# An mLSTM layer with a feed-forward network on one core: how the three-part operands of the late chunks are built

## Chip, core and metric

The kernel runs on one core of a Trainium2 chip. The metric is the device time of one execution in microseconds (us). TensorE is called PE in the profile, VectorE DVE, ScalarE ACT, GpSimd POOL, and SyncE, which issues nearly all DMAs, SP.

## The reference

Inputs are q, k, v and o_gate of shape (4, 8, 768, 40) (batch, heads, tokens, head size) and i_gate and f_gate of shape (4, 8, 768). Token by token, with a running maximum m that keeps the exponentials small:

```
m_new = max(f + m, i)
C = exp(f + m - m_new) * C + exp(i - m_new) * v k^T
n = exp(f + m - m_new) * n + exp(i - m_new) * k
y = sigmoid(o_gate) * (C q) / max(|n q|, 1)
```

The heads are joined to x of shape (3072, 320), and the network follows: h = x w_in (320 x 2048), g = max(h, 0) + alpha min(h, 0), out = g w_out (2048 x 320).

## The kernel before, in words

**Chunks and groups.** The recurrence is done in chunks of 128 tokens: 4 batches of NC = 6 chunks, n = 0 to 23. Two chunks (GC = 2) make a group of 256 tokens, and the network runs group by group, 12 groups. Within a chunk the weights between tokens are a masked matrix of scores (k against q, per head, times exponentials of the gates, tile E), and what came before the chunk enters through the state C.

**Precision.** Products are made from operands split into high and low parts. In the network x, the weights and g are split in two parts (XH and XL, WH and WL, OH and OL, gh and gl). In chunks n >= NDIR = 7, q and k are split into three bf16 parts, and the three parts of a head stand one above the other as 3 x 40 = 120 rows, so that one matmul adds three products of parts. Two such stacks of q, with the parts in other slots, against two of k give the six products that matter; `stage_b` (L410) issues the two matmuls per head at L443, and `from_state` (L358) does the same with stacks of q against two stacks of the state (L372).

**How the stacks are made now.** `token_parts(n, j)` (L220; j = 0 for q, 1 for k) fills a block by token, tile Z (names qZ and kZ): 128 tokens x 2 stacks x 8 heads x 128 columns, of which three slots of 40 hold the parts and 8 are zero (the memset at L231). ACT writes the first part to its slot in both stacks at once (L235). The remainder, tile `rest` (names qr and kr), is a subtraction at L236, for q on POOL and for k on DVE. ACT writes the second part (L238), DVE the third (L239), and DVE copies the first and the second part into the slots that are still open (L241, L242). One DMA transpose (L244) turns the block, 2048 columns, into the tile qS or kS with 120 rows in use. The block of q has the tag `sp0`, that of k the tag `sp1`, one buffer each, so a block can be written again only when the transpose of the chunk before has read it. The same two tags hold the split g of group 1 in the network's first part (names gg, L595). `stage_s` (L291) runs the two iterators: both first phases, a yield, the rest of q, a yield, the rest of k.

**State.** After each chunk `update_steps` (L149) and `state` (L184) bring C up to date, and from batch 1 on `state` splits it into three parts too, 40 rows of 336: ACT copies (L203, L205), a subtraction on DVE (L204) and one on POOL (L206), and three DMAs (L207 to L209) that place the parts in the other rows of the two stacks. The scratch tile `cw` shares the tag `qf` (two buffers) with `rest`.

**Order.** `attention` (L513) walks the chunks. In step n it issues `loads(n + 2)` (q, k, every second time v, and `load_L`, the row of gates that is spread over 128 partitions, 512 KB), runs `stage_s(n + 2)` as `far` and `stage_b(n)` as `bb`, and ends with `after(n + 1)`, which updates the state and splits v (`value_parts`, L317). The tuple at L524 says in which order their pieces come. The network of an earlier group is issued between these pieces (`ffn`, L646; `FeedForward.up`, L569; `down`, L603): per pair of blocks of 128 features `up` issues 16 matmuls into a buffer in PSUM (two buffers), ACT makes the negative part (L587), DVE the activation (L591, twice), ACT the high part gh (L599), POOL the low part gl (L600), and two pairs later `down` issues 12 matmuls (L608). Each engine carries out its queue in order. The order within a queue is set at build time by the framework's scheduler, which follows the program's order and may bring work forward that it reckons to be ready. The last two groups of the network run after the last chunk.

Of the kernel before, what the change touches and what calls it, by code (L numbers as in the profile page):

```python
# [8 lines left out]
F32 = mybir.dt.float32  # L9
F32R = mybir.dt.float32r  # L10
U32 = mybir.dt.uint32
BF16 = mybir.dt.bfloat16
# [5 lines left out]
def kernel(ctx: ExitStack, tc: tile.TileContext, q, k, v, i_gate, f_gate, o_gate, w_in, w_out, alpha, out):  # L18
    nc = tc.nc
# [75 lines left out]
    def by_token_of(n, j):  # L95

        t = (qn_t, kn_t)[j][n % NQ]
        if n < NDIR:
            return t[:, :, :D]
        return t.rearrange("p h e -> p (h e)")[:, : H * D].rearrange("p (h e) -> p h e", e=D)  # L100
# [83 lines left out]
    def state(n, pu):  # L184


        b, c = divmod(n, NC)
        C = C_t[0][:D]
        if c > 0:
            nc.gpsimd.tensor_tensor(  # L190
                C, C, gamB[:D, b * H : (b + 1) * H, c : c + 1].broadcast_to([D, H, VA]), ALU.mult
            )
        for par in range(2):
            to, new = by_parity(C, par), by_parity(pu[64 * par : 64 * par + D], par)
            if c == 0:
                nc.vector.tensor_copy(to, new)
            else:
                nc.vector.tensor_tensor(to, to, new, ALU.add)
        X = state_parts(n)
        C = C.rearrange("p h e -> p (h e)")  # L200
        cw = sb.tile([P, 512], F32, tag="qf", name=f"cw{n}")
        rest, low = cw[:D, : H * VA], cw[:D, H * VA :].bitcast(BF16)[:, : H * VA]
        nc.scalar.copy(X[:D, 0], C)  # L203
        nc.vector.tensor_tensor(rest, C, X[:D, 0], ALU.subtract)  # L204
        nc.scalar.copy(X[:D, 1], rest)  # L205
        nc.gpsimd.tensor_tensor(low, rest, X[:D, 1], ALU.subtract)  # L206
        nc.sync.dma_start(X[D : 2 * D], X[:D])  # L207
        nc.sync.dma_start(X[2 * D : 3 * D, 1], X[:D, 0])
        nc.sync.dma_start(X[2 * D : 3 * D, 0], low)  # L209

    def state_parts(n):

# [4 lines left out]
        for p in range(NPR):  # L217
            nc.tensor.transpose(ps[:R, p * P : (p + 1) * P], src[:, p * P : p * P + R], ident)

    def token_parts(n, j):  # L220

        src = by_token_of(n, j)
        Z = sb.tile([P, 2, H, P], BF16, tag=f"sp{j}", name=f"{'qk'[j]}Z{n}", bufs=1)
        rest = sb.tile([P, H, D], F32, tag="qf", name=f"{'qk'[j]}r{n}")

        def slot(block, i):
            return Z[:, block, :, i * D : (i + 1) * D]

        nc.gpsimd.memset(Z[:, :, :, 3 * D :], 0.0)  # L231
        flat = Z.rearrange("p s h x -> p (s h x)")
        W = H * P + 2 * D
        both = bass.AP(flat.tensor, flat.offset, [list(flat.ap[0]), [W, 2], [P, H], [1, D]])
        nc.scalar.copy(both, src.unsqueeze(1).broadcast_to([P, 2, H, D]))  # L235
        (nc.gpsimd, nc.vector)[j].tensor_tensor(rest, src, slot(0, 0), ALU.subtract)  # L236
        yield
        nc.scalar.copy(slot(1, 1), rest)  # L238
        nc.vector.tensor_tensor(slot(0, 2), rest, slot(1, 1), ALU.subtract)  # L239

        nc.vector.tensor_copy(slot(1 - j, 1 - (1 - j)), slot(0, 0))  # L241
        nc.vector.tensor_copy(slot(j, 1 - j), slot(1, 1))  # L242
        X = sb.tile([P, 2 * H, P], BF16, tag="qk"[j] + "S", name=f"{'qk'[j]}S{n}")
        nc.sync.dma_start_transpose(X, flat)  # L244
        stacks[n, j] = X.rearrange("p (s h) t -> p s h t", s=2)
        yield

    stacks = {}

    kpads = []  # L250

# [32 lines left out]
    def after(n):  # L284

        update(n)
        if n >= NBF:
            for _ in value_parts(n):
                pass

    def stage_s(n):  # L291

        parts = [token_parts(n, j) for j in range(2)]
        for it in parts:
            next(it)
        yield
        next(parts[0])
        yield
        next(parts[1])
        chunk[n] = (stacks.pop((n, 0)), stacks.pop((n, 1)), None)  # L300
        yield

    def values(n, E, busy=lambda: None):

# [53 lines left out]
    def from_state(n, qf, Q=None):  # L358

        b, c = divmod(n, NC)  # L360
        pI = psa(f"pI{n}")
        if b == 0:
            C = C_t[(n - 1) % 3][:R].rearrange("p h e -> p (h e)")
            for p in range(NPR):
                es = slice(2 * p * VA, 2 * (p + 1) * VA)
                nc.tensor.matmul(pI[:, es], qf[:R, p * P : (p + 1) * P], C[:, es], start=True, stop=True)
        else:
            C = state_parts(n - 1)[: 3 * D]
            for h in range(H):
                es = slice(h * VA, (h + 1) * VA)  # L370
                for s in range(2):
                    nc.tensor.matmul(pI[:, es], Q[: 3 * D, s, h], C[:, 1 - s, es], start=s == 0, stop=s == 1)  # L372
        yield
        T = sb.tile([P, H, VA], F32, tag="T", name=f"T{n}")
        nc.vector.tensor_tensor(
            T, pI[:, : H * VA].rearrange("p (h e) -> p h e", e=VA),
            eT[:, c, b * H : (b + 1) * H].unsqueeze(2).broadcast_to([P, H, VA]), ALU.mult,
        )
        yield T
# [30 lines left out]
    def stage_b(n):  # L410

        b, c = divmod(n, NC)
        Lb, (Q, K, qf) = pre.pop(n), chunk.pop(n)
        Es = []
        for par in range(2):
            E = sb.tile([P, 512], F32, tag="E", name=f"E{n}_{par}", bufs=4)
            if Lb is None:
                pb = psa(f"pb{n}_{par}")
                for p in range(NPR):
                    h = 2 * p + par  # L420
                    nc.tensor.matmul(
                        pb[:, p * P : (p + 1) * P], pick[:, h : h + 1].broadcast_to([3 * BH, P]),
                        LP[:, n % GC * P : (n % GC + 1) * P], start=True, stop=True,
                    )
            for p in range(NPR):
                h = 2 * p + par
                nc.scalar.activation(  # L427
                    E[:, p * P : (p + 1) * P], Lb[:, h] if Lb is not None else pb[:, p * P : (p + 1) * P], AF.Exp,
                    bias=bT[:, c, b * H + h : b * H + h + 1],
                )  # L430
            nc.gpsimd.affine_select(  # L431
                out=E, in_=E, pattern=[[0, NPR], [1, P]], base=0, channel_multiplier=-1,
                compare_op=ALU.is_ge, fill=0.0,
            )
            if c == 0 and par == 1:
                open_gate(b)
            pS = psa(f"pS{n}_{par}")
            for p in range(NPR):
                sl = slice(p * P, (p + 1) * P)
                if n >= NDIR:  # L440
                    h = 2 * p + par
                    for s in range(2):
                        nc.tensor.matmul(  # L443
                            pS[:, sl], K[: 3 * D, 1 - s, h], Q[: 3 * D, s, h], start=s == 0, stop=s == 1
                        )
                else:
                    nc.tensor.matmul(pS[:, sl], K[:R, par, sl], qf[:R, sl], start=True, stop=True)
            if n < NBF:
                nc.vector.tensor_tensor(E, pS, E, ALU.mult)
                Es.append(E)  # L450
            else:
                if par == 0:
                    E3 = late_pool.tile([P, 2, 512], BF16, tag="t", name=f"E3_{n}", bufs=3)
                Es.append(score_parts(pS, E, E3[:, par]))
            yield
        if c > 0:
            *_, T = from_state(n, qf, Q)
        hv = values(n, Es) if n < NBF else values_by_parts(n, Es)
        if c > 0:
            nc.vector.tensor_tensor(T, T, hv, ALU.add)  # L460
            hv = T
        gated(n, hv)
        if c == NC - 1 and n + 1 < B * NC:
            load_gate(b + 1, nc.sync)
        yield
# [40 lines left out]
    def loads(n):  # L506
        if n < B * NC:
            if n % GC == 0:
                load_v(n // GC)
            load_qk(n)  # L510
            pre[n] = load_L(n)

    def attention(n0):  # L513

        late = iter(())
        for _ in stage_a(n0):
            yield
        for n in range(n0, B * NC):
            loads(n + 2)
            a = stage_a(n + 1) if n + 1 < NDIR else iter(())  # L520
            far = stage_s(n + 2) if NDIR <= n + 2 < B * NC else iter(())
            bb = stage_b(n)

            for part in (a, bb, late, far, a, bb, far) + ((a, bb) if n + 1 < NC else (bb, a)):  # L524
                next(part, None)
                if part in (a, bb):
                    yield
            next(far, None)
            if NDIR <= n + 1 < B * NC:
                after(n + 1)  # L530
            if n % GC == GC - 1:
                late = stage_x(n // GC)
        for _ in late:
            yield
# [662 lines left out]
```

## Time and profile before

| what | value |
|---|---|
| median of three runs | 546.04 us (543.47 to 547.81) |
| the profiled execution, its own time | 543.58 us |
| its span, first to last instruction | 541.9 us |
| busy: PE, DVE, ACT, POOL | 496.4, 403.2, 326.7, 265.8 us |
| mean granted clock of TensorE | 0.962 |
| DMA queue of SP, share of 16 engines | 54.4%, 60.28 MB |

The profile is of one execution. Lines of instructions are grouped by source line, engine and tile; behind the bar stand the busy time of the group, the mean of one in ns, and the idle time of the engine just before them with what ended it. In the view of waits a row says which engine's line waited for which, the total in us, how often, and the longest. The chain of work that ended last gives start, duration and what it was. PEclk is the clock that TensorE was granted, 1.00 being full speed. An instruction's recorded time holds the time that it was held up while it ran.

### The profile page before, as it was taken

Reading aid. Unit: us, or ns where it says so; the run is one execution under the profiler, and the core shown is the slowest. Engines: PE = TensorE matmul, PEld = TensorE weight load, DVE = VectorE, ACT = ScalarE, POOL = GpSimd, SP = SyncE. Lnnn points to the kernel's source line nnn. Section 1 sums busy time; section 2 is a strip of 40 time slices with the busy share of each in tenths; the row PEclk is TensorE's granted clock in tenths of the full one; section 3 lists DMA queues with packets and bytes.
Section 4 is the critical chain, followed back from the end, with each engine's and each line's share of the span. In section 5 each row is a group of like instructions: output and inputs, shape, how many; then the busy total and the mean of one; then the engine's idle time right before and its main releaser. Section 6 shows DMA issues by size and latency. Waiting matters only on the chain.

```text
span 541.9 us, 11795 instructions
## 1 busy us (share of the span) xinstructions
PE 496.4 (92%) x4455; PEld 473.2 (87%) x4455; DVE 403.2 (74%) x782; ACT 326.7 (60%) x687; POOL 265.8 (49%) x336
## 2 busy tenths in 40 slices
PE   8879989997999889899998998799877999999997
PEld 7769989997999779788888897798777999999997
DVE  7889999464756789888699898889779787662321
ACT  3867897462585656676785574675765666533232
POOL 5722451211376457557566746646626646433232
PEclk9997979998999899899899999999997899999999
DMA  9989793624495763779474496657851360000000
GB/s 175 216 199 269 211 249 79 123 56 84 87 171 113 160 117 79 126 140 192 94 157 92 104 170 91 131 125 109 152 115 56 73 103 16 2 25 1 25 1 24
DMA packets 200770, 61.14 MB, mean 113 GB/s; under 512 B 171922, under 2 KB 197290, under 8 KB 200714
## 3 DMA queue, kind: packets, MB, share of 16 engines
q1 hardware_dynamic: 200634, 60.28, 54.4%
q8 instruction: 35, 0.57, 0.4%
q14 instruction: 21, 0.17, 0.1%
q10 hardware_dynamic: 80, 0.11, 0.1%
HBM read 36.90 MB, written 4.03 MB: 76 GB/s over the span
## 4 chain that ended last, share of the span: by engine, by line
PE 23%; DVE 20%; DMA 10%; ACT 7%; issue 3%; POOL 2%; ACTq 0%; POOLq 0%; SPq 0%; DVEq 0%
PE po L608 11%; DMA kS<-kZ 6%; DMA qS<-qZ 3%; DVE qZ L239 3%; DVE g L591 3%; DVE pS L333 2%; PE ph L578 1%; PE ph L580 1%; ACT E L427 1%; PE ph L581 1%; PE ph L584 1%; PE ph L582 1%; PE ph L583 1%; PE ph L585 1%; PE ph L579 1%
## 5 line engine op out<-in xcount | busy, mean ns | idle before, releaser
L600 POOL TENSOR_TENSOR gl<-g,gh 128x512 fp32r<-128x512 f32 x80 | 106.0, 1327 | 88.8 <-ACT gh L599 72.6
L608 PE MATMUL po<-OH,gh 128*128 128x320 f32 x352 | 109.5, 323 | 5.1 <-ACT gh L599 5.1
L608 PE MATMUL po<-OL,gh 128*128 128x320 f32 x352 | 106.8, 315 | 0.3 <-DVE OL L707 0.3
L591 DVE SCALAR_TENSOR_TENSOR g<-g,oma,ph 128x256 f32<-128x256 f32 x160 | 69.3, 472 | 44.1 <-ACT g L587 43.7
L587 ACT ACTIVATE g<-ph 128x512 f32<-128x512 f32 x96 | 57.1, 595 | 48.4 <-PE ph L585 36.7
L599 ACT CAST gh<-g 128x512 fp32r<-128x512 f32 x80 | 49.4, 619 | 39.8 <-DVE g L591 39.4
L608 PEld LDWEIGHTS po<-OH,gh 128*128 128x128 f32 x352 | 67.8, 193 | 5.9 <-ACT gh L599 5.7
L608 PE MATMUL po<-OH,gl 128*128 128x320 f32 x352 | 70.9, 323 | 2.2 <-POOL gl L600 2.2
L578 PE MATMUL ph<-XH,WH 128*128 128x256 f32 x192 | 59.9, 312 | 11.9 <-DVE g L591 7.3
L608 PEld LDWEIGHTS po<-OL,gh 128*128 128x128 f32 x352 | 67.7, 193 | 0.5 <-DVE OL L707 0.5
L608 PEld LDWEIGHTS po<-OH,gl 128*128 128x128 f32 x352 | 56.5, 194 | 2.6 <-POOL gl L600 2.5
L431 POOL TENSOR_SCALAR_AFFINE_SELECT E<-E 128x512 f32<-128x512 f32 x44 | 32.4, 738 | 53.5 <-ACT E L427 51.0
L582 PE MATMUL ph<-X,W 128*128 128x256 f32 x192 | 55.8, 291 | 0.0
L581 PE MATMUL ph<-XH,WL 128*128 128x256 f32 x192 | 55.7, 290 | 0.0
L584 PE MATMUL ph<-XL,WH 128*128 128x256 f32 x192 | 55.6, 290 | 0.0
L585 PE MATMUL ph<-X2L,W 128*128 128x256 f32 x192 | 55.5, 290 | 0.0
L583 PE MATMUL ph<-XL,WH 128*128 128x256 f32 x192 | 55.4, 289 | 0.0
L580 PE MATMUL ph<-XH,WL 128*128 128x256 f32 x192 | 55.4, 289 | 0.0
L579 PE MATMUL ph<-XH,WH 128*128 128x256 f32 x192 | 55.1, 287 | 0.0
L427 ACT ACTIVATE E<-Lb,bT 128x128 f32<-128x128 f32 x160 | 51.0, 393 | 3.0 <-PE pH L348 2.6
L335 ACT CAST E<-pS 128x512 bf16<-128x512 f32 x64 | 37.3, 583 | 23.4 <-DVE pS L333 12.2
L578 PEld LDWEIGHTS ph<-XH,WH 128*128 128x128 f32 x192 | 37.3, 194 | 13.5 <-DVE gg L600 4.6
(199 smaller groups left out, 1246.3 us busy)
## 6 DMA issues: line engine op xcount, KB each, us to landing
Lb<-L_d SPq DMA_DIRECT2D x20, 512.0 KB
wo<-in_moe_w_out_dram SPq DMA_DIRECT2D x8, 640.0 KB
wi<-in_moe_w_in_dram SPq DMA_DIRECT2D x8, 512.0 KB
qn<-in_q_dram SPq DMA_DIRECT2D x24, 160.0 KB
kn<-in_k_dram SPq DMA_DIRECT2D x24, 160.0 KB
va<-in_v_dram SPq DMA_DIRECT2D x24, 160.0 KB
og<-in_o_gate_dram SPq DMA_DIRECT2D x24, 160.0 KB
out_dram<-ob SPq DMA_DIRECT2D x11, 320.0 KB
```

What stands on the lines that cost most here:

```text
L578: nc.tensor.matmul(dst, WH[half][:, 0, hs], XH[:, 0], start=True, stop=False)
L579: nc.tensor.matmul(dst, WH[half][:, 1, hs], XH[:, 1], start=False, stop=False)
L580: nc.tensor.matmul(dst, WL[half][:, 0, hs], XH[:, 0], start=False, stop=False)
L581: nc.tensor.matmul(dst, WL[half][:, 1, hs], XH[:, 1], start=False, stop=False)
L582: nc.tensor.matmul(dst, W2[:, fs], X2, start=False, stop=False)
L583: nc.tensor.matmul(dst, WH[half][:, 0, hs], XL[:, 0], start=False, stop=False)
L584: nc.tensor.matmul(dst, WH[half][:, 1, hs], XL[:, 1], start=False, stop=False)
L585: nc.tensor.matmul(dst, W2[:, fs], X2L, start=False, stop=True)
L587: nc.scalar.activation(gt, ph, AF.Relu, scale=-1.0)
L591: nc.vector.scalar_tensor_tensor(out=y[:, e], in0=gt[:, e], scalar=oma[:, f : f + 1], in1=ph[:, e], op0=ALU.mult, op1=ALU.add)
L600: (nc.vector if g < 2 else nc.gpsimd).tensor_tensor(gl, y, gh.bitcast(F32), ALU.subtract)
L608: nc.tensor.matmul(po[j], x[:, e, j * P : (j + 1) * P], W[f // NB][:, f % NB], **ends)
```

## The change

The two blocks by token become one, Z, with the parts of q in its first half and those of k in its second, each only once. It has the tag `sp0` for even n and `sp1` for odd n. Two transposes of 1024 columns each make the second stack (`X[:, 1]`) of q and of k. The first stack (`X[:, 0]`) is made from the second by four DMAs in a new function `shifted`, which move two slots by one and copy one slot back (q and k in opposite directions); they are issued at the start of the step after. All four subtractions of q and k are on POOL, the copies on DVE are gone, and ACT's first cast writes one slot and no longer two. In `state` the high part goes to the scratch tile and its subtraction to POOL, and the DMAs are divided otherwise. The stacks of k and C are in the order that q's have, so L372 and L443 lose their `1 - s`. `load_L(n + 2)` moves from the start of step n to behind its sixth piece. `stage_s` is gone, and `far` has two pieces, no longer three.

```diff
@@ -199,14 +199,14 @@
         X = state_parts(n)
         C = C.rearrange("p h e -> p (h e)")
         cw = sb.tile([P, 512], F32, tag="qf", name=f"cw{n}")
-        rest, low = cw[:D, : H * VA], cw[:D, H * VA :].bitcast(BF16)[:, : H * VA]
-        nc.scalar.copy(X[:D, 0], C)
-        nc.vector.tensor_tensor(rest, C, X[:D, 0], ALU.subtract)
-        nc.scalar.copy(X[:D, 1], rest)
-        nc.gpsimd.tensor_tensor(low, rest, X[:D, 1], ALU.subtract)
-        nc.sync.dma_start(X[D : 2 * D], X[:D])
-        nc.sync.dma_start(X[2 * D : 3 * D, 1], X[:D, 0])
-        nc.sync.dma_start(X[2 * D : 3 * D, 0], low)
+        rest, high = cw[:D, : H * VA], cw[:D, H * VA :].bitcast(BF16)[:, : H * VA]
+        nc.scalar.copy(high, C)
+        nc.gpsimd.tensor_tensor(rest, C, high, ALU.subtract)
+        nc.scalar.copy(X[:D, 0], rest)
+        nc.gpsimd.tensor_tensor(X[:D, 1], rest, X[:D, 0], ALU.subtract)
+        nc.sync.dma_start(X[D : 2 * D, 0], high)
+        nc.sync.dma_start(X[2 * D : 3 * D], high.unsqueeze(1).broadcast_to([D, 2, H * VA]))
+        nc.sync.dma_start(X[D : 2 * D, 1], X[:D, 0])
     def state_parts(n):
@@ -217,35 +217,39 @@
         for p in range(NPR):
             nc.tensor.transpose(ps[:R, p * P : (p + 1) * P], src[:, p * P : p * P + R], ident)
-    def token_parts(n, j):
-        src = by_token_of(n, j)
-        Z = sb.tile([P, 2, H, P], BF16, tag=f"sp{j}", name=f"{'qk'[j]}Z{n}", bufs=1)
-        rest = sb.tile([P, H, D], F32, tag="qf", name=f"{'qk'[j]}r{n}")
-        def slot(block, i):
-            return Z[:, block, :, i * D : (i + 1) * D]
+    def token_parts(n):
+        Z = sb.tile([P, 2, H, P], BF16, tag=f"sp{n % 2}", name=f"Z{n}", bufs=1)
         nc.gpsimd.memset(Z[:, :, :, 3 * D :], 0.0)
-        flat = Z.rearrange("p s h x -> p (s h x)")
-        W = H * P + 2 * D
-        both = bass.AP(flat.tensor, flat.offset, [list(flat.ap[0]), [W, 2], [P, H], [1, D]])
-        nc.scalar.copy(both, src.unsqueeze(1).broadcast_to([P, 2, H, D]))
-        (nc.gpsimd, nc.vector)[j].tensor_tensor(rest, src, slot(0, 0), ALU.subtract)
-        yield
-        nc.scalar.copy(slot(1, 1), rest)
-        nc.vector.tensor_tensor(slot(0, 2), rest, slot(1, 1), ALU.subtract)
-        nc.vector.tensor_copy(slot(1 - j, 1 - (1 - j)), slot(0, 0))
-        nc.vector.tensor_copy(slot(j, 1 - j), slot(1, 1))
-        X = sb.tile([P, 2 * H, P], BF16, tag="qk"[j] + "S", name=f"{'qk'[j]}S{n}")
-        nc.sync.dma_start_transpose(X, flat)
-        stacks[n, j] = X.rearrange("p (s h) t -> p s h t", s=2)
+        src, rest, slots = [], [], []
+        for j in range(2):
+            src.append(by_token_of(n, j))
+            rest.append(sb.tile([P, H, D], F32, tag="qf", name=f"{'qk'[j]}r{n}"))
+            slots.append([Z[:, j, :, i * D : (i + 1) * D] for i in ((0, 1, 2), (2, 1, 0))[j]])
+            nc.scalar.copy(slots[j][0], src[j])
+        for j in range(2):
+            nc.gpsimd.tensor_tensor(rest[j], src[j], slots[j][0], ALU.subtract)
+        yield
+        for j in range(2):
+            nc.scalar.copy(slots[j][1], rest[j])
+            nc.gpsimd.tensor_tensor(slots[j][2], rest[j], slots[j][1], ALU.subtract)
+            X = sb.tile([P, 2, H, P], BF16, tag="qk"[j] + "S", name=f"{'qk'[j]}S{n}")
+            nc.sync.dma_start_transpose(X[:, 1], Z[:, j].rearrange("p h x -> p (h x)"))
+            stacks[n, j] = X
         yield
     stacks = {}
+    def shifted(n):
+        Q, K = (stacks.pop((n, j)) for j in range(2))
+        nc.sync.dma_start(Q[D : 3 * D, 0], Q[: 2 * D, 1])
+        nc.sync.dma_start(K[: 2 * D, 0], K[D : 3 * D, 1])
+        nc.sync.dma_start(Q[:D, 0], Q[:D, 1])
+        nc.sync.dma_start(K[2 * D : 3 * D, 0], K[2 * D : 3 * D, 1])
+        chunk[n] = (Q, K, None)
     kpads = []
@@ -287,18 +291,6 @@
         if n >= NBF:
             for _ in value_parts(n):
                 pass
-    def stage_s(n):
-        parts = [token_parts(n, j) for j in range(2)]
-        for it in parts:
-            next(it)
-        yield
-        next(parts[0])
-        yield
-        next(parts[1])
-        chunk[n] = (stacks.pop((n, 0)), stacks.pop((n, 1)), None)
-        yield
     def values(n, E, busy=lambda: None):
@@ -369,7 +361,7 @@
             for h in range(H):
                 es = slice(h * VA, (h + 1) * VA)
                 for s in range(2):
-                    nc.tensor.matmul(pI[:, es], Q[: 3 * D, s, h], C[:, 1 - s, es], start=s == 0, stop=s == 1)
+                    nc.tensor.matmul(pI[:, es], Q[: 3 * D, s, h], C[:, s, es], start=s == 0, stop=s == 1)
         yield
         T = sb.tile([P, H, VA], F32, tag="T", name=f"T{n}")
         nc.vector.tensor_tensor(
@@ -441,7 +433,7 @@
                     h = 2 * p + par
                     for s in range(2):
                         nc.tensor.matmul(
-                            pS[:, sl], K[: 3 * D, 1 - s, h], Q[: 3 * D, s, h], start=s == 0, stop=s == 1
+                            pS[:, sl], K[: 3 * D, s, h], Q[: 3 * D, s, h], start=s == 0, stop=s == 1
                         )
                 else:
                     nc.tensor.matmul(pS[:, sl], K[:R, par, sl], qf[:R, sl], start=True, stop=True)
@@ -508,7 +500,6 @@
             if n % GC == 0:
                 load_v(n // GC)
             load_qk(n)
-            pre[n] = load_L(n)
     def attention(n0):
@@ -516,16 +507,19 @@
         for _ in stage_a(n0):
             yield
         for n in range(n0, B * NC):
+            if NDIR <= n + 1 < B * NC:
+                shifted(n + 1)
             loads(n + 2)
             a = stage_a(n + 1) if n + 1 < NDIR else iter(())
-            far = stage_s(n + 2) if NDIR <= n + 2 < B * NC else iter(())
+            far = token_parts(n + 2) if NDIR <= n + 2 < B * NC else iter(())
             bb = stage_b(n)
-            for part in (a, bb, late, far, a, bb, far) + ((a, bb) if n + 1 < NC else (bb, a)):
+            for i, part in enumerate((a, bb, late, far, a, bb, far) + ((a, bb) if n + 1 < NC else (bb, a))):
                 next(part, None)
+                if i == 5 and n + 2 < B * NC:
+                    pre[n + 2] = load_L(n + 2)
                 if part in (a, bb):
                     yield
-            next(far, None)
             if NDIR <= n + 1 < B * NC:
                 after(n + 1)
             if n % GC == GC - 1:
```

## The prediction

> **What bounds the kernel now.** I read the page first: PE is busy 92% of the span, so time can only come from PE's idle time, from its clock, or from less work on PE, and the change touches no product. Second, the busy time by stretches, cut where the late chunks begin and where attention ends (columns: stretch, then busy us of PE, PEld, DVE, ACT, POOL with instruction counts, PEclk, DMA share, GB/s).
>
> ```profile
> 106.00:475.00 369.00, 336.11 (x3179) 321.82 (x3178) 292.41 (x561) 231.61 (x490) 201.93 (x253) 0.96 0.56 108
> 475.00:542.00 67.00, 63.55 (x497) 63.17 (x494) 19.62 (x45) 20.58 (x36) 22.86 (x19) 1.00 0.04 16
> ```
>
> The second stretch is the network alone, at full clock: nothing to win. In the first, the only one that the change touches, PE is idle 369.0 - 336.1 = 32.9 us and runs at 0.96. With no idle time and full clock it would take 336.1 x 0.96 = 322.7 us, so the most that any relief can give is 46 us. Third, whom PE waits for in that stretch:
>
> ```profile
> PE ph L578 <- DVE g L591: 7.3, 6, 2.3
> PE pH L348 <- ACT E L335: 5.2, 3, 2.6
> PE po L608 <- ACT gh L599: 4.6, 3, 1.9
> PE ph L578 <- DVE gg L600: 4.5, 1, 4.5
> PE p L471 <- DVE xn L403: 3.8, 3, 2.4
> PE po L608 <- POOL gl L600: 2.2, 2, 2.0
> PE pI L372 <- DVE E L336: 2.0, 1, 2.0
> ```
>
> PE waits for the ends of chains that run through DVE and ACT. What makes those late is in the chain of work that ended last, and in the timeline of one such place:
>
> ```profile
> 190.60 3.23 DVE qZ L239
> 199.18 4.30 DMA kS<-kZ
> 217.47 5.73 DMA kS<-kZ
> ```
>
> ```profile
> 411.38 3.95 DVE L239 TENSOR_TENSOR qZ<-qr,qZ 128x320 bf16<-128x320 f32 x1
> ```
>
> ```profile
> 411.05 0.72 POOL L401 TENSOR_TENSOR og<-og,r 128x320 f32<-128x320 f32 x1
> 411.73 1.28 POOL L600 TENSOR_TENSOR gl<-g,gh 128x512 fp32r<-128x512 f32 x1
> 412.98 0.77 POOL L326 TENSOR_TENSOR vb<-vr,vb 128x336 bf16<-128x336 f32 x1
> 413.72 1.25 POOL L600 TENSOR_TENSOR gl<-g,gh 128x512 fp32r<-128x512 f32 x1
> ```
>
> At 411.38 a DVE subtraction whose operands all lie in SBUF takes 3.95 us and ends at 415.33, a little after POOL's run of four two-input operations (411.05 to 414.97). It is held until POOL pauses, with all of DVE's queue behind it; the 2.0 us wait of L372 follows. The Trainium skill (SBUF — State Buffer, "Who interferes with whom") calls the port pair that the two share an exclusive lock, which a DVE operation with two SBUF inputs meets; this trace agrees (3.95 us).
>
> **The change part by part.** *DVE.* These are the groups of the stretch that go, and three that stay:
>
> ```profile
> L239 DVE TENSOR_TENSOR qZ<-qr,qZ 128x320 bf16<-128x320 f32 x17 | 22.7, 1336 | 4.9 <-ACT qZ L238 4.8
> L204 DVE TENSOR_TENSOR cw<-C,C 40x336 f32<-40x336 f32 x15 | 13.9, 928 | 0.0
> L236 DVE TENSOR_TENSOR kr<-kn,kZ 128x320 f32<-128x320 f32 x17 | 12.7, 746 | 0.0
> L403 DVE TENSOR_TENSOR xn<-T,og 128x320 f32<-128x320 f32 x13 | 12.1, 929 | 0.3 <-POOL og L401 0.2
> L239 DVE TENSOR_TENSOR kZ<-kr,kZ 128x320 bf16<-128x320 f32 x17 | 10.7, 631 | 0.7 <-ACT kZ L238 0.7
> L460 DVE TENSOR_TENSOR T<-T,S 128x336 f32<-128x336 f32 x13 | 10.1, 781 | 0.1
> L242 DVE COPY kZ<-kZ 128x320 bf16<-128x320 bf16 x17 | 8.8, 515 | 0.0
> L242 DVE COPY qZ<-qZ 128x320 bf16<-128x320 bf16 x17 | 8.1, 475 | 0.0
> L241 DVE COPY kZ<-kZ 128x320 bf16<-128x320 bf16 x17 | 8.0, 472 | 15.3 <-ACT kZ L235 15.3
> L375 DVE TENSOR_TENSOR T<-pI,eT 128x336 f32<-128x336 f32 x15 | 7.5, 497 | 0.0
> ```
>
> The quoted groups that go have 22.7 + 13.9 + 12.7 + 10.7 + 8.8 + 8.1 + 8.0 = 84.9 us of DVE's 292.4, and 4.9 + 0.7 + 15.3 = 20.9 us of idle time. How much of it is being held? L375, as large but with one input in PSUM, takes 497 ns; over that stand L239 (1336 + 631 - 994) x 17 = 16.5, L204 (928 - 497) x 15 = 6.5 and L236 (746 - 497) x 17 = 4.2 us, together 27.2. What stays of the kind is L403 (929 - 497) x 13 = 5.6 and L460 (781 - 497) x 13 = 3.7, together 9.3. So 27.2 / 36.5 = 75% of the held time goes; with the copies, which are held too, I say 80%.
>
> *ACT and the buffers.* Rows of ACT's waits, and one of its groups:
>
> ```profile
> ACT kZ L235 <- DMA kS<-kZ: 17.4, 11, 3.0
> ACT kZ L238 <- DVE kr L236: 15.6, 7, 4.0
> ACT qZ L235 <- DMA qS<-qZ: 8.0, 8, 1.9
> ACT qZ L238 <- POOL qr L236: 1.6, 3, 0.9
> L235 ACT CAST kZ<-kn 128x640 bf16<-128x640 f32 x17 | 12.3, 723 | 18.5 <-DMA kS<-kZ 17.4 <-PE po L608 1.0
> ```
>
> The two L235 waits are for a transpose that still reads the only block. With blocks that alternate, the reader is a whole chunk back: 25.4 us go, and ACT has gh (L599) behind them. The wait for kr moves to POOL, where the same wait for q is 1.6, so 15.6 becomes about 3. The casts shrink from 640 to 320 columns, worth some 0.25 us each, hidden under PE.
>
> *PE's idle time.* The rows L591, gh, gl and pI of PE's waits, 7.3 + 4.6 + 2.2 + 2.0 = 16.1 us, are DVE and ACT being late; by the 80% I take 12.9 off (bounds: half, 8.0, and all, 16.1). The 4.5 us before gg is the transposes of the first late chunk holding the tags of gg; as Z now holds one tag and not two, I take half, 2.3 (bounds 0 and 4.5). E (5.2) and xn (3.8) I leave. Sum: 15.2 of 32.9 us, 46%.
>
> *Clock.* 0.96 costs 0.04 x 336.1 = 13.4 us in this stretch, and the stretch without idle time has 1.00. I let the clock come back in the same proportion, 46%: 6.2 us (bounds 0 and 13.4).
>
> *POOL.* What is added is priced by these:
>
> ```profile
> L236 POOL TENSOR_TENSOR qr<-qn,qZ 128x320 f32<-128x320 f32 x17 | 14.5, 851 | 1.4 <-ACT qZ L235 1.4
> L206 POOL TENSOR_TENSOR cw<-cw,C 40x336 bf16<-40x336 f32 x15 | 12.8, 855 | 0.0
> L600 POOL TENSOR_TENSOR gl<-g,gh 128x512 fp32r<-128x512 f32 x63 | 84.1, 1337 | 50.8 <-ACT gh L599 39.6 <-issue 7.4 <-PE pH L348 2.7
> ```
>
> Three more subtractions per chunk, 3 x 17 x 0.85 = 43.4, and one per state, 15 x 0.855 = 12.8: 56 us, less one small memset per chunk. POOL goes from 202 to about 256 of 369 us, 55% to 69%, and 167 us of idle time cover it: PE waits for POOL only 2.2 us today. The cost is longer runs, which hold L403 and L460. Their 9.3 us may double; DVE's 85 + 21 us came with 12.9 us of PE, so 9.3 more cost about 1. With later gl I take +2 (bounds 0 and +10: DVE's extra passed on whole). The Trainium skill (GPSIMD Engine Reference, "4.1 Engine selection") advises VectorE for two-input work, GpSimd being about twice as slow. In this queue the row for k on DVE has 746 ns, that for q on POOL 851. By the skill's ratio on 497 ns the 66 operations would cost 66 us (an estimate) and not 56, which POOL's idle time would cover too.
>
> *SP and the DMAs.* Rows of SP's issues, then a load on the chain, then the readers of kS:
>
> ```profile
> L244 SPq DMA_TRANSPOSE qS<-qZ x17: 1624/2632/3684, 119.4 to 441.1; - x17
> L244 SPq DMA_TRANSPOSE kS<-kZ x17: 1799/2022/3243, 123.2 to 439.2; - x17
> L207 SPq DMA_DIRECT2D C<-C x15: 709/747/772, 122.2 to 448.0; - x15
> ```
>
> ```profile
> 388.31 2.65 DMA qn<-in_q_dram
> ```
>
> ```profile
> L443 PE MATMUL pS<-qS,kS x272: 216/219/330, 128.7 to 470.4; 120*128 120x128 bf16 x136
> ```
>
> Transposes of half the columns should take half of 2.6 and 2.0 us to issue: -2.3 per chunk (bounds 0 and -2.3); four slot moves at 0.75: +3.0. That is +0.7 us of SP per chunk, which nothing waits for unless the order of the queue makes it (the last rival). The moves' landing is not in the trace: 160 KB of short rows from memory land in 2.65 us, and the transposes in 4.3 to 5.7; I take 2.65, half a transpose more at most. It lies after the transposes and before L443. The last pair starts at 441.1 and its last reader at 470.4, so there is room; the first k transpose lands at about 127.5 (issued at 123.2, 4.3 to land) and its first reader starts at 128.7, so there is none. I charge +1 us once (bounds 0 and +4). The moved row of gates comes two pieces later for a reader two steps on: nothing. The state's DMAs remain three.
>
> **Sum.** -15.2 - 6.2 + 2 + 1 = -18.4 us. The profiled execution took 543.6, so 525.2; the median of the runs lies 2.5 above it, 546.0, so I predict 546.0 - 18.4 = **527.6**. The likeliest case's own range, from its bounds taken partly together, is 511 to 538.
>
> **Rivals.** *PE almost without gaps.* If E and xn were late for the same cause, nearly all 32.9 us and most of the clock go, 36 of the 46 us: 510. For it: every long wait ends in DVE or ACT. Against: L348 and L471 wait behind work that stays.
>
> *POOL sets the pace.* POOL now works 256 us, and of its 167 idle us 50.8 stand before gl in the row above; with as much again before its other work (an estimate), 100 us are waits for other engines that no freed block removes; 34 third parts each wait for an ACT cast between two POOL steps, some 0.3 us, 10 us more. 256 + 100 + 10 = 366 of 369: gain 3, so 543. Against: waits shrink when ACT is earlier.
>
> *SP blocks the loads: slower.* `shifted(n + 1)` stands ahead of the loads of q and k for n + 2, and its first DMA waits for the transposes. If SP arrives before they land, the loads start late, ACT's cast waits for them, and gh and E behind it. ACT's longest wait for a transpose, 3.0, left PE 2.3 idle, so a wait W costs about W - 0.7. Over 17 chunks the gain is used up at W = 1.8 us; at 3.0, the four issues, it is 17 x 2.3 - 18.4 = +20.7: 567, and 551 at W = 2.1. For it: SP's order is fixed. Against: loads may be brought ahead of the moves, and a chunk has 20 us.
>
> **Numbers.** Forecast 0.50, gap-free PE 0.14, POOL's pace 0.27, SP 0.09. A measurement of this kernel tells about 1% (5.5 us) from no change. Faster by over 1%: 0.50 + 0.14 + 0.16 of POOL's 0.27 = 0.80; within: 0.11; slower: 0.09. Range 508 to 544: below lies half of the gap-free case, above the SP case and the weakest of POOL's.
>
> **What would show it.** Right: DVE near 210 us busy in the stretch, ACT's waits for transposes gone, PE idle under 20 us, PEclk 0.98, POOL near 256 us at 0.85 each. Wrong: L403 and L460 above 1.2 us, PE waiting for gl, ACT waiting for qn or kn, or PE as idle as before behind other names.

## The result and the profile after

The changed kernel takes 514.4 us (median of four runs, 513.59 to 514.61) against 544.75 us: ratio 0.9435, 95% interval 0.9385 to 0.9485. Predicted were 527.6 us, 18.4 us less; measured are 30 us less. Here and below the ratios leave out single runs over 1.5% slower than the fastest of their kernel, the medians keep them. The profiled execution took 514.26 us, with a span of 512.5 (541.9 before).

To compare equal work I cut both spans at the first and the ninth store of an output (118.9 and 444.9 us before, 125.4 and 415.1 after; columns as in the prediction). The kernel before, then the changed one:

```profile
0.00:118.90 118.90, 109.69 (x889) 100.81 (x890) 99.19 (x196) 83.40 (x174) 42.98 (x68) 0.94 0.77 175
118.90:444.90 326.00, 293.21 (x2785) 279.90 (x2784) 262.19 (x499) 204.97 (x443) 184.17 (x232) 0.96 0.61 118
```

```profile
0.00:125.40 125.40, 115.74 (x904) 106.97 (x905) 99.54 (x195) 84.30 (x178) 46.98 (x73) 0.92 0.78 175
125.40:415.10 289.70, 281.11 (x2768) 269.64 (x2767) 192.41 (x366) 194.99 (x439) 217.49 (x275) 0.99 0.57 126
415.10:512.50 97.40, 93.38 (x789) 92.36 (x785) 42.36 (x89) 38.02 (x71) 39.72 (x37) 1.00 0.07 22
```

The middle stretch is 326.0 - 289.7 = 36.3 us shorter. PE's idle time in it fell from 326.0 - 293.2 = 32.8 to 289.7 - 281.1 = 8.6 us, which is 24.2; PE's busy time fell by 12.1, at a clock of 0.99 for 0.96, with 17 instructions less in the stretch. The traces say how much of the 12.1 is the clock: in the middle stretch it was at 0.50 for 27.3 us before, in seven pieces of 3.4 or 6.8 us, and for 6.8 us after, in one piece. Half of that time is lost, 13.65 and 3.41 us, so the clock gives back some 10.2 us (an estimate). One such piece, before:

```profile
180.50:183.90 3.40, 3.40 (x18) 3.12 (x16) 2.17 (x5) 1.96 (x6) 0.79 (x2) 0.50 1.13 230
```

All seven pieces begin within 1.3 us of the end of a pause of PE of 1.8 to 4.5 us (the one shown follows a pause of 1.93 us that ends at 179.2); pauses of 1.95, 2.08 and 2.37 us elsewhere in the stretch are not followed by one. By these traces a wait of PE can cost more than its own length. The first stretch is 6.5 us longer, the last 0.4: together 29.4, the difference of the spans. DVE works 70 us less in the middle stretch. Whom PE now waits for in the middle stretch, all rows:

```profile
PE p L463 <- DVE xn L395: 2.7, 1, 2.7
PE pH L340 <- ACT E L327: 2.5, 2, 1.8
PE ph L572 <- DVE r L390: 1.6, 1, 1.6
PE ph L572 <- DVE g L585: 0.9, 3, 0.4
PE po L602 <- POOL gl L594: 0.7, 1, 0.7
```

The waits for g, gh, gg and the state's product are gone or nearly so. L595 to L608 of before are L589 to L602 here, and most other lines moved too. ACT's waits for the transposes and for POOL's remainders in the same stretch:

```profile
ACT Z L230 <- DMA kS<-Z: 8.2, 6, 1.7
ACT Z L230 <- DMA qS<-Z: 5.7, 3, 2.1
ACT Z L235 <- POOL qr L232: 4.9, 6, 1.7
ACT Z L235 <- POOL kr L232: 3.4, 4, 1.6
```

ACT's waits for transposes fell from 25.4 to 13.9 us, not to nothing; POOL, which zeroes the 8 free columns of the block, waited 30.2 us for them before and waits 17.8 us now. Next the two DVE groups that were to be held more, and three of POOL's new groups, of the same stretch:

```profile
L395 DVE TENSOR_TENSOR xn<-T,og 128x320 f32<-128x320 f32 x11 | 17.1, 1554 | 1.8 <-POOL og L393 1.6
L452 DVE TENSOR_TENSOR T<-T,S 128x336 f32<-128x336 f32 x11 | 8.8, 800 | 0.2
```

```profile
L236 POOL TENSOR_TENSOR Z<-kr,Z 128x320 bf16<-128x320 f32 x16 | 12.8, 797 | 5.7 <-ACT Z L235 5.6
L232 POOL TENSOR_TENSOR kr<-kn,Z 128x320 f32<-128x320 f32 x16 | 12.7, 791 | 0.2 <-DMA C<-cw 0.2
L204 POOL TENSOR_TENSOR cw<-C,cw 40x336 f32<-40x336 f32 x13 | 11.5, 882 | 0.0
```

xn is held as foreseen, 1554 ns for 929. That is above the 1.2 us which the prediction named as a sign of being wrong; it cost PE little, as the wait for xn is 2.7 us and was 3.8. POOL's prices are the predicted ones, 0.80 for 0.85. Last SP: the issue of a transpose, and its waits at the slot moves:

```profile
L238 SPq DMA_TRANSPOSE qS<-Z x17: 1234/1274/2338, 114.8 to 410.6; - x17
```

```profile
SPq L248 <- DMA qS<-Z: 12.0, 10, 2.8
SPq L249 <- DMA kS<-Z: 11.4, 8, 2.9
```

Half the columns take 1.27 us to issue, for 2.63 (q) and 2.02 (k). SP does stand 23.4 us before the slot moves, which was the condition of the rival that ended slower, but hardly anyone waits for it: no row of PE, no load of q or k among ACT's waits, and 0.6 us for a load of k among POOL's, as before. The loads of q and k wait longer for POOL, which still reads the tiles that they fill:

```profile
SPq L93 <- POOL qr L232: 18.9, 4, 15.1
SPq L93 <- POOL kr L232: 12.8, 7, 3.4
```

### The profile page after: what moved, and what is told of

Its sections match the earlier page's. It is cut to its first block, busy times and chain, and to the rows that moved or that the text cites. A ratio compares the mean times of both kernels' runs of the same rounds, so it can differ in the third digit from the quotient of the medians.

```text
span 512.5 us, 11748 instructions
## 1 busy us (share of the span) xinstructions
PE 490.2 (96%) x4455; PEld 469.0 (91%) x4455; DVE 334.3 (65%) x648; ACT 317.3 (62%) x687; POOL 304.2 (59%) x385
## 4 chain that ended last, share of the span: by engine, by line
PE 67%; DVE 9%; POOL 8%; DMA 6%; ACT 4%; issue 4%; SPq 1%; ACTq 0%; POOLq 0%; DVEq 0%
PE po L602 25%; PE ph L572 4%; PE ph L578 3%; PE ph L575 3%; PE ph L573 3%; PE ph L576 3%; PE ph L577 3%; PE ph L574 3%; PE ph L579 3%; DMA kS<-Z 2%; POOL gl L594 2%; PE pH L340 2%; PE warm L929 2%; DMA wo<-in_moe_w_out_dram 2%; PE pS L435 2%
## 5 line engine op out<-in xcount | busy, mean ns | idle before, releaser
L594 POOL TENSOR_TENSOR gl<-g,gh 128x512 fp32r<-128x512 f32 x80 | 103.8, 1297 | 60.9 <-ACT gh L593 51.4
L602 PE MATMUL po<-OH,gh 128*128 128x320 f32 x352 | 107.8, 318 | 0.5 <-ACT gh L593 0.5
L602 PE MATMUL po<-OL,gh 128*128 128x320 f32 x352 | 105.2, 311 | 0.0
L602 PE MATMUL po<-OH,gl 128*128 128x320 f32 x352 | 68.8, 316 | 0.7 <-POOL gl L594 0.7
L602 PEld LDWEIGHTS po<-OH,gh 128*128 128x128 f32 x352 | 66.6, 190 | 1.0 <-ACT gh L593 0.9
L602 PEld LDWEIGHTS po<-OL,gh 128*128 128x128 f32 x352 | 66.4, 189 | 0.2 <-DVE OL L701 0.2
L423 POOL TENSOR_SCALAR_AFFINE_SELECT E<-E 128x512 f32<-128x512 f32 x44 | 31.3, 713 | 42.3 <-ACT E L419 39.2
L602 PEld LDWEIGHTS po<-OH,gl 128*128 128x128 f32 x352 | 55.0, 190 | 1.2 <-POOL gl L594 1.1
L578 PE MATMUL ph<-XL,WH 128*128 128x256 f32 x192 | 54.8, 286 | 0.0
L575 PE MATMUL ph<-XH,WL 128*128 128x256 f32 x192 | 54.7, 285 | 0.0
L577 PE MATMUL ph<-XL,WH 128*128 128x256 f32 x192 | 54.6, 285 | 0.0
L574 PE MATMUL ph<-XH,WL 128*128 128x256 f32 x192 | 54.6, 284 | 0.0
```

Source lines behind the costliest of these rows:

```text
L574: nc.tensor.matmul(dst, WL[half][:, 0, hs], XH[:, 0], start=False, stop=False)
L575: nc.tensor.matmul(dst, WL[half][:, 1, hs], XH[:, 1], start=False, stop=False)
L577: nc.tensor.matmul(dst, WH[half][:, 0, hs], XL[:, 0], start=False, stop=False)
L578: nc.tensor.matmul(dst, WH[half][:, 1, hs], XL[:, 1], start=False, stop=False)
L594: (nc.vector if g < 2 else nc.gpsimd).tensor_tensor(gl, y, gh.bitcast(F32), ALU.subtract)
L602: nc.tensor.matmul(po[j], x[:, e, j * P : (j + 1) * P], W[f // NB][:, f % NB], **ends)
```

## The experiments

**The theories.** Theory 1: the gain is DVE's queue, which is shorter and less held. Theory 2: the gain is the block that alternates, with shorter transposes. The ratios below are to the kernel before on the same chip, with 95% intervals.

**One half of the change alone.** `b_subs_pool`, on the kernel before:

```diff
-        nc.vector.tensor_tensor(rest, C, X[:D, 0], ALU.subtract)
+        nc.gpsimd.tensor_tensor(rest, C, X[:D, 0], ALU.subtract)
-        (nc.gpsimd, nc.vector)[j].tensor_tensor(rest, src, slot(0, 0), ALU.subtract)
+        nc.gpsimd.tensor_tensor(rest, src, slot(0, 0), ALU.subtract)
-        nc.vector.tensor_tensor(slot(0, 2), rest, slot(1, 1), ALU.subtract)
+        nc.gpsimd.tensor_tensor(slot(0, 2), rest, slot(1, 1), ALU.subtract)
```

> The kernel before, with only the three subtractions of q, k and the state that DVE did given to GpSimd; blocks, copies, transposes and the row of gates as before. Theory 1 (the gain is DVE no longer being held on operands in SBUF): most of the 30 us come from this alone, 522 to 530 us, DVE 50 us less busy. Theory 2 (the gain is the block that alternates and the shorter transposes, so that ACT no longer waits for a transpose): at most 8 us, 537 to 545, and ACT still waits 20 us or more for transposes.

523.3 us, ratio 0.9587 (0.9525 to 0.9649). Its middle stretch, and its waits for transposes:

```profile
120.90:423.00 302.10, 284.76 (x2772) 272.69 (x2767) 225.40 (x433) 203.94 (x443) 222.56 (x294) 0.98 0.65 126
```

```profile
ACT kZ L235 <- DMA kS<-kZ: 15.8, 9, 4.0
ACT qZ L235 <- DMA qS<-qZ: 10.3, 9, 1.8
```

23 us come from the subtractions alone, while ACT waits 26.1 us for transposes, as much as ever (23.0 in the same window before). So the gain doesn't need those waits to go. DVE is 37 us less busy, not 50. Then `a_subs_dve`, the changed kernel with the subtractions back:

```diff
-        nc.gpsimd.tensor_tensor(rest, C, high, ALU.subtract)
+        nc.vector.tensor_tensor(rest, C, high, ALU.subtract)
-            nc.gpsimd.tensor_tensor(rest[j], src[j], slots[j][0], ALU.subtract)
+            (nc.gpsimd, nc.vector)[j].tensor_tensor(rest[j], src[j], slots[j][0], ALU.subtract)
-            nc.gpsimd.tensor_tensor(slots[j][2], rest[j], slots[j][1], ALU.subtract)
+            nc.vector.tensor_tensor(slots[j][2], rest[j], slots[j][1], ALU.subtract)
```

> The changed kernel, with those subtractions (k's remainder, both third parts, the state's remainder) back on DVE; alternating blocks, half transposes, slot moves and no copies stay. Theory 1: most of the gain is lost, 530 to 540 us, and the subtractions on DVE are again held, 0.7 us or more on average. Theory 2: little is lost, 515 to 522.

519.8 us, ratio 0.9514 (0.9470 to 0.9558): most of the gain stays, with DVE's subtractions held again:

```profile
122.60:419.90 297.30, 283.73 (x2765) 270.83 (x2763) 232.09 (x427) 196.16 (x439) 181.37 (x214) 0.98 0.56 124
```

```profile
L236 DVE TENSOR_TENSOR Z<-qr,Z 128x320 bf16<-128x320 f32 x16 | 16.0, 1002 | 2.0 <-ACT Z L235 2.0
```

Here Theory 1, as written, missed, and the time is the one that Theory 2 gave: most of the gain is there without the subtractions. But the copies are off DVE here too. The two halves don't add up, each gives most of the whole.

**One buffer for the block.** `a_one_block`:

```diff
-        Z = sb.tile([P, 2, H, P], BF16, tag=f"sp{n % 2}", name=f"Z{n}", bufs=1)
+        Z = sb.tile([P, 2, H, P], BF16, tag="sp0", name=f"Z{n}", bufs=1)
```

> The changed kernel with one buffer for the block of parts in place of two. Theory 1: 514 to 520 us, as a transpose of half the columns frees the block early enough. Theory 2: 525 to 540, and ACT and GpSimd wait for the transposes 20 us or more again.

512.95 us, ratio 0.9384 (0.9337 to 0.9432), a little below Theory 1's range. ACT waits for transposes no longer than with two buffers:

```profile
ACT Z L230 <- DMA kS<-Z: 6.4, 4, 2.9
ACT Z L230 <- DMA qS<-Z: 4.9, 4, 1.9
```

POOL waits 22.3 us for them, with two buffers 17.8. The second buffer is worth nothing here. `a_subs_dve_one` is the same edit on top of `a_subs_dve`:

> The changed kernel with the subtractions back on DVE and one buffer for the block. If DVE's load alone sets the pace: as with two buffers, 517 to 523 us. If the second buffer matters once DVE is loaded: 526 to 540, with ACT waiting 20 us or more for transposes.

530.3 us, ratio 0.9741 (0.9679 to 0.9802): with DVE loaded, the second buffer is worth 0.9741 - 0.9514, some 12 us. DVE is as busy as in `a_subs_dve`, but ACT waits 18.5 us for transposes from 120 to 420 us, where `a_subs_dve` has 10.4:

```profile
120.20:434.60 314.40, 288.24 (x2796) 274.20 (x2795) 233.40 (x435) 199.22 (x447) 180.51 (x217) 0.98 0.57 121
```

```profile
ACT Z L230 <- DMA qS<-Z: 12.3, 7, 3.5
ACT Z L230 <- DMA kS<-Z: 6.2, 5, 1.5
```

So DVE's load isn't all: at 232 and 233 us of it the gain is 4.9% and 2.6%. What a second buffer would give the kernel before, with its larger blocks, has no run and stays open.

**DVE's load as before, with the new blocks.** `a_full_dve` has the edits of `a_subs_dve` and, behind each third part, two copies without use:

```diff
+            for i in (0, 1):
+                again = sb.tile([P, H, D], BF16, tag="again", name=f"again{n}_{j}{i}", bufs=1)
+                nc.vector.tensor_copy(again, slots[j][i])
```

> The changed kernel with the subtractions back on DVE and, as extra work with no use, four copies of 320 bf16 per chunk on DVE into a scratch tile, so that DVE's queue holds what it held before; alternating blocks, half transposes and slot moves stay. If DVE's load is what set the pace: 538 to 546 us. If the blocks and the transposes do a large part by themselves: 515 to 525.

533.4 us, ratio 0.9801 (0.9739 to 0.9863): neither number, nearer to the first.

```profile
121.90:433.20 311.30, 286.05 (x2766) 272.92 (x2765) 254.48 (x491) 195.60 (x439) 180.67 (x214) 0.98 0.54 118
```

```profile
L239 DVE COPY again<-Z 128x320 bf16<-128x320 bf16 x64 | 34.5, 539 | 2.2 <-ACT Z L230 2.1
```

With DVE at 254 of 311 us the gain is 10 us, so by this run DVE's load is worth about 20 of the 30; the rest is blocks, transposes, loads and the order of the instructions (below). The reverse is `b_copies_pool`, the kernel before with only the copies on POOL:

```diff
-        nc.vector.tensor_copy(slot(1 - j, 1 - (1 - j)), slot(0, 0))
-        nc.vector.tensor_copy(slot(j, 1 - j), slot(1, 1))
+        nc.gpsimd.tensor_copy(slot(1 - j, 1 - (1 - j)), slot(0, 0))
+        nc.gpsimd.tensor_copy(slot(j, 1 - j), slot(1, 1))
```

> The kernel before, with only DVE's four copies per chunk given to GpSimd; subtractions, blocks and transposes as before. If taking either half of the moved work off DVE is enough for PE to come near its own bound: 520 to 530 us. If the subtractions, which read two operands from SBUF and are held, are the half that counts: 538 to 546.

520.0 us, ratio 0.9522 (0.9436 to 0.9607), though DVE's third part of q is held nearly as before and ACT still waits for kr:

```profile
L239 DVE TENSOR_TENSOR qZ<-qr,qZ 128x320 bf16<-128x320 f32 x16 | 19.7, 1232 | 0.2 <-ACT qZ L238 0.2
L238 ACT CAST kZ<-kr 128x320 bf16<-128x320 f32 x17 | 7.8, 457 | 15.5 <-DVE kr L236 15.4
```

So the holding of these subtractions is no cause by itself: with 32 us less in DVE's queue (230 of 304 us busy) PE's idle time in the stretch is 16.7 us for 32.8, with those holds in place. ACT's waits for transposes fell there too, from 23.0 to 10.2 us from 120 to 420 us, so this run doesn't part DVE's load from them; `b_subs_pool` does.

**The moved load.** `a_gates_early` puts `pre[n] = load_L(n)` back into `loads`.

> The changed kernel with the load of the row of gates back at the start of the step. Both theories: within 1% of the changed kernel, 512 to 519 us. If the load's place is a part of the gain by its own (SP waits there for ACT's exponentials, 40.8 us in the kernel before), it is 520 or more.

512.8 us, ratio 0.9378 (0.9317 to 0.9439): the place of the load is worth nothing that can be measured.

**What is left, and POOL's room.** `a_xn_pool` sets `XNP = range(2, 24)`; `a_xn_again` is the same kernel once more; `a_xn_t_pool` has `T = T + S` of n >= NBF on POOL besides; `a_again` is the changed kernel itself.

> The changed kernel with the product of the gate (xn) on GpSimd in all chunks: it is now the DVE work that is held most, 1554 ns on average, and PE's longest wait of the late stretch, 2.7 us, is for it. If what is left of PE's idle time is DVE held behind GpSimd: 508 to 512 us. If not: 513 to 517, the same.

> The changed kernel as it is, once more, for a second profile and for a direct comparison: 512 to 516 us. If the 4.5 us by which the profiled execution was late in its first 40 us belong to the change, this profile has them too; if they are chance, it need not.

> The changed kernel with xn on GpSimd in all chunks, once more: 505 to 510 us, with an interval that lies below that of the changed kernel.

> The same with the sum T = T + S on GpSimd as well, the last large DVE operation that reads two operands from SBUF. If being held is still worth something: 502 to 506 us. If PE is at its bound, or GpSimd, now the step before xn, is late: 505 to 512.

`a_xn_pool`: 506.9 us, 0.9320 (0.9257 to 0.9383). Later, on another chip, `a_again` has 512.2 us, 0.9355 (0.9293 to 0.9418), `a_xn_again` 508.2, 0.9324 (0.9272 to 0.9377), `a_xn_t_pool` 507.7, 0.9318 (0.9267 to 0.9368). By the ratios xn on POOL is 1.7 to 2.0 us better than `a_again`, and the intervals overlap, which was not expected: not settled. Then `a_pool_more`, which issues work without use, on the changed kernel:

```diff
+            for i in (0, 1):
+                again = sb.tile([P, H, D], BF16, tag="again", name=f"again{n}_{j}{i}", bufs=1)
+                nc.gpsimd.tensor_tensor(again, rest[j], slots[j][1], ALU.subtract)
```

> The changed kernel with four subtractions per chunk more on GpSimd into a scratch tile, work with no use: some 51 us in the late stretch, GpSimd at about 268 of 290 us. If GpSimd has room beside PE: 514 to 520 us. If the rival that GpSimd sets the pace begins here: 525 or more.

502.2 us, ratio 0.9237 (0.9178 to 0.9296), below both expected ranges and the lowest median of all; its interval just meets that of `a_again`. Its stretches:

```profile
120.60:402.30 281.70, 278.66 (x2723) 268.26 (x2723) 189.13 (x359) 191.39 (x428) 249.73 (x317) 1.00 0.57 125
402.30:500.20 97.90, 94.07 (x837) 92.46 (x836) 49.43 (x98) 42.78 (x84) 56.42 (x61) 1.00 0.15 38
```

POOL is busy 250 of 282 us and PE idle for 3.0: POOL doesn't set the pace even there. Useless work can hardly help by itself; what else differs is the order of the instructions. PE carries out the same 4455 matmuls in both kernels, the first 893 in the same order and the rest in another (the two profiles of the changed kernel agree throughout). PE waits less, and the clock is never at 0.50 in the middle stretch. The last stretch holds 837 of PE's instructions for 789: attention reaches further into the network's end, and the middle is shorter. That the order is the cause is thus argued, not shown by a run of its own. The scheduler that sets the order at build time reckons with the work it is given, so each kernel here has an order of its own. That also bounds the readings above: a difference of 1 to 2% between two kernels may be order. What in that order helps stays open.

## Why the prediction was right, and what it sized wrongly

The direction and the range (508 to 544) hold, and the mechanism in the main: what DVE no longer does is what PE no longer waits for. The size was 18.4 for 30. By steps:

- **Waits for DVE and ACT (g, gh, gl, pI: 16.1, of which 12.9 taken off).** Measured 0.9 + 0.7 left and a new 1.6 for r: 3.2, so 12.9 gone. The step is right in size. Its reason, held operations, is only half right: `b_copies_pool` gains 23 us with the subtractions still held. It is the length of DVE's queue in the main, with the block's buffers where DVE is loaded (`a_subs_dve_one`).
- **gg (4.5, half taken).** All of it went: no such row is left. `b_subs_pool` and `b_copies_pool`, with the old blocks, still have 3.5 and 4.8 us of it.
- **E and xn (5.2 and 3.8, left as they were).** This is the step that failed. They were 9.0 us and are 5.2, so 3.8 went, and three rows of before that the sum left out, 3.1 us, are gone too; 12.9 + 4.5 + 3.8 + 3.1 = 24.3 is the idle time that PE lost. These waits, too, hang on DVE, if not wholly: in `b_copies_pool`, which relieves DVE alone, the rows of E are 1.3 and 0.7 us and that of xn 0.6. They should have been counted in part. The three rows:

```profile
PE pH L348 <- DVE XL L493: 1.7, 2, 1.5
PE pH L348 <- ACT gh L599: 1.0, 1, 1.0
PE pH L348 <- DVE E L336: 0.4, 1, 0.4
```

- **Clock (6.2).** Measured 10.2, with 1.9 more of PE's busy time that is not the clock; 17 instructions at 281.1 / 2768 = 0.10 us each make 1.7 of it (an estimate). The proportion came out here: 74% of the idle time went, and 75% of the lost clock (13.65 to 3.41 us) came back. The term was too small because the idle time in it was. As a rule the proportion is loose: in `a_full_dve` PE is still idle 25.3 us, 23% less, and half of the lost clock is back (13.65 us at 0.50, for 27.3).
- **POOL (+2) and the first chunk (+1).** POOL's 56 us became 38 over the span (304.2 for 265.8 busy): the added operations took some 53, the memsets that went gave back 3.5, and most other operations got a little shorter (gl 1297 ns for 1327, xn's copy 326 for 403). It cost PE nothing visible: the sum of the two rows in which PE waits for POOL or for xn is 3.4 us, and was 6.0. Around the first late chunk, from 100 to 145 us, PE waits for nothing. `a_pool_more` puts the rival that POOL sets the pace aside up to 250 of 282 us.
- **The rival of SP.** Its condition is there, its effect isn't. The moves do stand ahead of loads in SP's queue (moves at 178.4 to 180.5 us, the next load of q at 184.2), but the loads are for two chunks on, and waited longer for POOL than SP did for the transposes (31.7 us for 23.4).
- **The rival of PE almost without gaps (0.14)** came close to what happened in the middle stretch: 36.3 us, the rival's 36 of at most 46. What it had against it, "L348 and L471 wait behind work that stays", held in part: 5.2 us of these waits are left. That the whole gain is 30 and not 36 us is the longer first stretch.

What wasn't in the sum: 6.5 us more in the first stretch, of which some 5 don't belong to the change, below. Without them the gain of the profiled execution would be 34 us, so the forecast was further off than the times alone say.

## What to carry to other kernels

DVE was busy 262 of 326 us here, 80%, and less work on it took away waits of PE that were put down to ACT and POOL too (gh 4.6 to none, gl 2.2 to 0.7). So count all waits that end at such an engine or at its neighbours, and not only those whose rows name a piece that goes. Reliefs of such an engine don't add: 23 us for the subtractions alone, 23 for the copies alone (26 by the ratio) and 30 for the whole change, since PE had only 32.8 us of idle time in the stretch, of which the halves took 15.5 and 16.1. And a buffer that is worth nothing at a light load (`a_one_block`) was worth 12 us at a heavier one (`a_subs_dve_one`). And with an order set at build time, an edit is never alone: compare several variants before a per cent is put down to one of them.

## What was not expected of the hardware

The same program began in two ways. The changed kernel's profile and `a_again`, from 20 to 30 us, and the first product there:

```profile
20.00:30.00 10.00, 10.00 (x63) 9.53 (x64) 6.77 (x12) 5.62 (x9) 4.93 (x5) 0.55 1.17 171
```

```profile
20.42 3.18 PE L304 MATMUL pH<-va,E 128*128 128x42 f32 x16
```

```profile
20.00:30.00 10.00, 9.49 (x86) 8.48 (x81) 9.45 (x22) 6.01 (x12) 5.08 (x6) 1.00 1.20 174
```

```profile
20.03 1.98 PE L304 MATMUL pH<-va,E 128*128 128x42 f32 x16
```

At a mean granted clock of 0.55 (0.50 from 21.0 to 31.2 us) the same 16 matmuls take 3.18 us for 1.98, and the first split of x comes at 33.7 us for 29.0. The 4.7 us stay: the first store comes at 125.4 us and in `a_again` at 120.4. Of the 14 profiles kept, four have 0.52 to 0.56 in these 10 us, two have 0.83 and eight 1.00, the kernel before among them. Both executions have an idle time of PE of 1.7 us just before (in front of L161), so that alone doesn't decide it. The Trainium skill (TensorE: Matmul & The Clock Gate, "Part 1: The HAM clock gate (the "warmup" mystery)") has the array at half its clock after an idle window of about 3.4 us, and the window runs freely, so that the point of change varies from run to run. The traces agree with the half clock (0.50) and with the varying, but not with the length of the pause: no idle time of PE of 3.4 us stands before the half clock here, it followed a pause of 1.7 us in one execution and not in another. PE's first 893 matmuls come in the same order before and after the change, and the same program has both beginnings, so this part of the longer first stretch is chance.
